# A fused attention and mixture-of-experts kernel: products with v from float16 parts, 240 slots per expert, weight conversion shared between two stages

## The chip, the cores and the metric

The kernel runs on one core of one Trainium2 chip, as one launch. The metric is the device time of one execution in microseconds (us); smaller is better. The core has a matrix engine (TensorE: PE for its products, PEld for its weight loads), three engines for elementwise work (VectorE, DVE; ScalarE, ACT; GpSimd, POOL) and a queue engine (SyncE, SP) that issues most of the transfers. Each engine works through its own list of instructions in order, and semaphores hold it where it needs another's result.

## The reference

```
# attention, batch 2, 8 heads, 768 positions, head size 64
mask   = bucket(q) == bucket(k)          # 6 sign bits of x @ proj
scores = where(mask, q @ k.T / 8, -1e9)
x      = softmax(scores) @ v             # -> 1536 tokens of 512
# dense layer, 512 -> 2048 -> 512
h = x @ w_in;  x = (h * tanh(softplus(h))) @ w_out
# eight experts, 512 -> 1024 -> 512; each token goes to one of them
e   = argmax(cosine(x, expert_emb) / tau)
out = softmax(...)[e] * (relu(x @ w1[e]) @ w2[e])
```

Everything is float32 in the arguments and in the result.

## The kernel before

All products but one kind are made from float16 parts: each float32 operand is cut into a high part and a low part, and three float16 products (high by high, high by low, low by high) are added up in PSUM. The one exception is the product of the softmax numerators `p` with `v` (`pv`), which takes float32 operands. The kernel has three stages.

**Attention** (16 heads, one after another). The work of a head is cut into 6 steps, one for each tile of 128 keys; `g` counts the steps, 6 to a head, and each step has 6 positions. In a step TensorE makes the scores of one key tile (`score_unit`, L384 and L386, two halves of 384 queries each), one or two products for the row maxima of a head that comes 10 steps later (`max_unit`, L344 and L348; VectorE reduces each out of PSUM, two buffers, L345 and L349), and the two products of the tile of 3 steps before with `v` (`pv`, L401). ScalarE makes `p` from the scores (L389). `AT` says at which position, counted from a head's first step, each of the other pieces is issued: the cut of q and k into parts (`hi`, `lo0`, `lo1`), the transposing transfers on SP's queue (`in_x`, `in_m`), the bucket bits (`args`, `bits`), and for each pair of heads the normalisation (`inv`, `scale`, `xhi`, `xlo`). `run_all` writes this order out, and a helper keeps each engine to it.

**Dense layer** (3 chunks of 512 tokens, 16 tiles of 128 hidden columns, so 48 tiles `G`). For each tile TensorE makes 12 products `up` (L767) and, three tiles later, 12 products with `w_out` (L825). Between them four ScalarE functions, three VectorE operations (L846, L851, L867), one ScalarE copy (L860) and one GpSimd subtraction (L861) make the two parts of `g`. `w_in` and `w_out` come as float64 and are converted by `w1_work`: 32 pieces of 128 x 512, each with three VectorE operations (L694, L696, L676: these are the steps of the generator), then ScalarE and GpSimd operations for the two parts (`w1_free` in the attention, `w1_busy` in the dense layer, where the low parts of `w_out` are left to VectorE). `CVS` says how many steps of that generator are taken in each step `g` of the attention; the rest is taken in the dense layer by `fill`, which is called 6 times a tile and takes one step when the generator is due (what it yields says how many calls must pass). The conversion for expert 0 (`w2_work`, L1105 and L1106) is chained behind it.

**Experts**. A table in DRAM has `CAP` slots for each expert; tokens are scattered to it, and every expert works on all its slots: for each expert 96 products `up` with `CAP` columns (L1150) and 48 products `down` with 512 columns, whose weights are the hidden values of 128 slots (L1164). The weights of the next expert are loaded and cut meanwhile (L1087, L646, L647). If an expert had more tokens than `CAP`, a fallback loop over all experts and all tokens would run (`overflow`).

Of the kernel before, what the change touches and what calls it, by code (L numbers as in the profile page):

```python
# [11 lines left out]
F16 = mybir.dt.float16  # L12
# [8 lines left out]
P = 128  # L21
# [6 lines left out]
PB = 5  # L28
EMB0 = -2
BLANK = 4  # L30
CVS = ((5, 99, 1),)
LEAD = 5
UP = {95: 0, 99: 1}
TEND = 101
PRE = {96: 2, 97: 2, 98: 2}
RPB, CVB = 1, 3
STEP = 7
AT = dict(rows_t=-7, rows_in=-7, m_row=-22, bits=-90, max_end=-24, hi=-150, lo0=-130, lo1=-122, dup=-114, in_x=-116, in_m=-84, args=-91, load_kq=-190, load_v=-37, out0=50, out1=54, s_row=55, inv=77, r_out=79, r_in=91, scale=112, xhi=127, xlo=139)
GAP = dict(bits=1, max_end=1, inv=1)
STEPS = dict(bits=3, max_end=2, inv=2)  # L40
FROM = dict(rows_in=1, m_row=4, bits=3, max_end=1, hi=4, lo0=4, lo1=4, dup=4, in_x=4, in_m=4, rows_t=1, args=3, load_kq=6, load_v=2)
UNTIL = dict(rows_t=4, rows_in=4)
EVERY = dict(load_kq=(2, 0), load_v=(2, 0)) | {k: (2, 1) for k in ("inv", "r_out", "r_in", "scale", "xhi", "xlo")}
LAST = ("inv", "r_out", "r_in", "scale", "xhi", "xlo")
SP, MP, OP = 1, (1, 5, 11), (1, 5)
NBUF, NVB, KXB, KMB = 3, 2, 5, 4
# [97 lines left out]
class Attn:  # L144
    def __init__(self, tc, ctx, q, k, v, proj, ident, ones, xx, dt, rest):
# [42 lines left out]
        for i in range(PB):  # L188
            if i in (1, 2):
                p = self.two[:, (i - 1) * (S + 1) : i * (S + 1)]  # L190
            else:
                p = self.pp.tile([P, S + 1], F32, name=f"p{i}", bufs=1)
            nc.gpsimd.memset(p[:, S : S + 1], 1e-9 / S)
            self.PT.append(p)

# [131 lines left out]

    def load_v(self, b, h):
# [48 lines left out]
    def score_unit(self, b, h, t):  # L377
# [9 lines left out]
        p = self.PT[self.pt % PB]  # L387
# [4 lines left out]
    def pv(self, b, h, t, c):  # L392
# [7 lines left out]
        o = z["o", c][0:m, 0 : HS + c]  # L400
        nc.tensor.matmul(o, self.vn(b, h, t), z["p"][t][:, cs], start=(t == 0), stop=(t == NJ - 1))  # L401

    def wide(self, b, h, tag, bufs):

        last = b == B - 1 and h >= H - 2
        name = tag
        pool, tag, bufs = (self.rest_pools[0], "stg", None) if last else (self.ou, tag, bufs)
        return pool.tile([P, S + 1], F32, tag=tag, name=f"{name}_{b}_{h}", bufs=bufs)

    def out(self, b, h, c):  # L410
# [13 lines left out]
        if i:  # L424
            self.nc.scalar.copy(z["s"][:, cs], o[0:1, 0:HS])

# [40 lines left out]
    def run_all(self, bs, hook=None):  # L467
# [47 lines left out]
        for n in range(N):  # L515
            for name, at in AT.items():
# [6 lines left out]
                if name in GAP:  # L523
# [56 lines left out]
CAP = 256  # L580
# [19 lines left out]
class Moe:  # L600
# [32 lines left out]
    def blank(self, tp, i):  # L633
# [6 lines left out]
        n = E0 * CAP // P // 16  # L640
        dst = self.xs[i * n * P : (i + 1) * n * P, :].rearrange("(a p) c -> p a c", p=P)
        nc.sync.dma_start(dst, self.z[:, None, :].to_broadcast([P, n, ROW]))
# [22 lines left out]
    def w1_work(self):  # L665
# [18 lines left out]
        for k in range(2 * NF1 + 1):  # L684
            busy = self.busy
            if old:
                end()
                yield 1
            if k < 2 * NF1:
# [5 lines left out]
                yield 1  # L695
                nc.vector.scalar_tensor_tensor(x, high, 0xC0000000, x, op0=ALU.bitwise_and, op1=ALU.bitwise_or)  # L696
                yield 1
# [683 lines left out]
```

## Time and profile before

| | |
|---|---|
| runs of the kernel before | 687.63 us median of 3 (686.86 to 688.06) |
| the profiled execution | 688.07 us; its span, first to last instruction, 686.3 us |
| granted TensorE clock over the span | 0.996 |
| busy, share of the span | PE 98%, PEld 54%, DVE 64%, ACT 69%, POOL 22% |

Busy is the union of an engine's instructions; a share is an average over stages that have different limits, so it has to be read stage by stage. The span leaves out 1.8 us around the first and the last instruction.

### The profile page before, as it was taken

To read this page: it belongs to the slowest core of one execution; us is meant where nothing else is said; L and a number is where in the kernel's file an instruction comes from. 1 tells how busy PE (TensorE), PEld (TensorE's weight loads), DVE (VectorE), ACT (ScalarE), POOL (GpSimd) and SP (SyncE) were. 2 spreads that over 40 slices of the span, in tenths; PEclk is the share of its full clock that TensorE was granted. 3 is DMA by queue.
4 is the path that set the end of the run, shared out by engine and by line. 5 is a ranking of instruction groups with operands and counts; after the bars stand their busy time and mean duration, and the time that the engine had idled before them with its cause. 6 is when DMAs were issued, how large, how long until landed. Compare 5 with 4: busy or idle time off the path is not lost. (4 is left out here: it accounts for less than half of the span.)

```text
span 686.3 us, 10415 instructions
## 1 busy us (share of the span) xinstructions
PE 670.8 (98%) x3890; PEld 371.5 (54%) x3890; DVE 440.9 (64%) x747; ACT 472.2 (69%) x716; POOL 152.7 (22%) x166
## 2 busy tenths in 40 slices
PE   8899999999999999999999999999999999999994
PEld 4555555555555454444444444445476777666772
DVE  6877888898887546766675555445466565556520
ACT  5667677676766769999898778887655565555520
POOL 3131211121111122222243242532530011110011
PEclk9999999999999999999999999999999999999998
DMA  7276887978864412345031010310555999988500
GB/s 218 64 148 151 183 194 165 229 156 186 179 136 134 118 56 91 91 125 154 1 98 26 1 63 22 78 24 2 187 181 145 305 275 292 251 258 245 157 23 21
DMA packets 120939, 93.23 MB, mean 136 GB/s; under 512 B 87847, under 2 KB 100135, under 8 KB 120882
## 3 DMA queue, kind: packets, MB, share of 16 engines
q1 hardware_dynamic: 112610, 81.18, 45.7%
q0 software_dynamic: 2240, 6.31, 3.3%
q10 hardware_dynamic: 6032, 5.01, 2.8%
q8 instruction: 32, 0.52, 0.3%
q14 instruction: 25, 0.20, 0.1%
HBM read 63.47 MB, written 14.77 MB: 114 GB/s over the span
## 5 line engine op out<-in xcount | busy, mean ns | idle before, releaser
L401 PE MATMUL o<-p,vn 128*65 128x384 f32 (+3 forms) x384 | 153.3, 486 | 0.1
L767 PE MATMUL h<-xx,wi 128*128 128x512 f16 x576 | 131.3, 379 | 0.1
L825 PE MATMUL x<-wo,g 128*128 128x512 f16 x576 | 131.2, 379 | 0.0
L389 ACT ACTIVATE p<-s 128x768 f32<-128x768 f32 x96 | 77.5, 808 | 53.0 <-PE s L386 51.3
L825 PEld LDWEIGHTS <-g 128*128 128x128 f16 x576 | 56.2, 98 | 68.1 <-POOL g L861 0.3
L767 PEld LDWEIGHTS <-wi 128*128 128x128 f16 x576 | 56.0, 98 | 67.5 <-issue 0.8
L861 POOL TENSOR_TENSOR g<-w,g 128x512 f16<-128x512 f32 x47 | 55.1, 1173 | 149.6 <-ACT g L860 90.4
L1164 PE MATMUL y<-b,hh 128*128 128x512 f16 x384 | 84.2, 379 | 0.0
L1150 PEld LDWEIGHTS <-a 128*128 128x128 f16 x768 | 75.1, 98 | 10.4 <-issue 0.2
L345 DVE TENSOR_REDUCE mx<-ms 128x1 f32<-128x512 f32 x96 | 65.8, 688 | 15.8 <-PE ms L344 15.2
L1150 PE MATMUL h<-xt,a 128*128 128x256 f16 x672 | 74.5, 273 | 0.0
L867 DVE SCALAR_TENSOR_TENSOR w<-w,u 128x512 f32<-128x512 f32 x47 | 32.5, 692 | 64.0 <-ACT u L858 64.0
L401 PEld LDWEIGHTS o<-p,vn 128*65 128x65 f32 (+1 forms) x384 | 59.6, 163 | 24.8 <-issue 10.8
L1164 PEld LDWEIGHTS <-hh 128*128 128x128 f16 x384 | 37.6, 98 | 43.6
L846 DVE SCALAR_TENSOR_TENSOR t<-t,u 128x512 f32<-128x512 f32 x47 | 39.1, 832 | 22.2 <-ACT t L873 22.2
L647 DVE SCALAR_TENSOR_TENSOR b<-st,b 128x1024 f16<-128x1024 f32 x28 | 33.1, 1222 | 24.8 <-ACT b L646 24.5
L1169 POOL DMA_INDIRECT out_dram<-o,row x16 | 15.6, 973 | 150.1 <-ACT o L1168 128.9
L647 DVE SCALAR_TENSOR_TENSOR a<-st,a 128x1024 f16<-128x1024 f32 x28 | 34.3, 1226 | 21.9 <-ACT a L646 21.9
L386 PE MATMUL s<-tm 97*128 97x384 f16 x192 | 47.0, 325 | 0.0
L384 PE MATMUL s<-tx 128*128 128x384 f16 x192 | 46.8, 325 | 0.0
L349 DVE TENSOR_REDUCE mx<-ms 128x2 f32<-128x512 f32 x48 | 33.0, 688 | 16.0 <-PE ms L348 15.3
L1156 ACT ACTIVATE hh<-h 128x512 f16<-128x512 f32 x32 | 19.1, 596 | 34.2 <-PE h L1150 33.1
(185 smaller groups left out, 917.6 us busy)
## 6 DMA issues: line engine op xcount, KB each, us to landing
st<-in_moe_w_dram SPq DMA_DIRECT2D x32, 1024.0 KB, 6.2
stg<-in_moe_w_in_dram SPq DMA_DIRECT2D x16, 512.0 KB, 4.2
stg<-in_moe_w_out_dram SPq DMA_DIRECT2D x16, 512.0 KB, 4.3
xs<-zrow SPq DMA_DIRECT2D x16, 257.0 KB, 8.1
vn<-in_v_dram SPq DMA_DIRECT2D x16, 192.0 KB, 6.5
rb<-rd SPq DMA_DIRECT2D x16, 192.0 KB, 3.7
xr<-row SPq DMA_DIRECT2D x2, 1024.0 KB
kq<-in_k_dram ACTq DMA_DIRECT2D x5, 384.0 KB, 3.9
```

Source lines behind the costliest of these rows:

```text
L345: nc.vector.tensor_reduce(z["mx"][:, j, 0:1], s, axis=AX.X, op=ALU.max)
L384: nc.tensor.matmul(s[:, c, :], kq[:, 0, ts], kq[:, 1, c * HS : (c + 1) * HS], start=True, stop=False)
L386: nc.tensor.matmul(s[:, c, :], m[0:97, 0, ts], m[0:97, 1, c * HS : (c + 1) * HS], start=False, stop=True)
L389: nc.scalar.activation(p[:, 0:S].rearrange("p (c n) -> p c n", c=2), s, AF.Exp, scale=2.0**-11)
L401: nc.tensor.matmul(o, self.vn(b, h, t), z["p"][t][:, cs], start=(t == 0), stop=(t == NJ - 1))
L647: nc.vector.scalar_tensor_tensor(lo, src, sc, hi, op0=ALU.mult, op1=ALU.subtract)
L767: self.nc.tensor.matmul(h, self.wi[wu][:, k, fs], x[:, k, xs], start=(i == 0), stop=(i == 3 * NKT - 1))
L825: nc.tensor.matmul(x2[r], gf[:, gu, rs], self.wo[wu][:, f, :], start=(f == 0 and gu + wu == 0), stop=(f == NF1 - 1 and gu == 1))
L846: nc.vector.scalar_tensor_tensor(t1, t1, 0.75, u1, op0=ALU.add, op1=ALU.mult)
L861: nc.gpsimd.tensor_tensor(g[G - 1][:, 1, :], p1, g[G - 1][:, 0, :], op=ALU.subtract)
L1150: nc.tensor.matmul(h[:, v, :], W[0][wu][:, k, fs], xt[e][:, xu * NKT + k, :], start=(i == 0), stop=(i == 3 * NKT - 1))
L1164: nc.tensor.matmul(y[s], hs[F // 2][:, hu, F % 2, s * P : (s + 1) * P], W[1][wu][:, F, :], start=(F == 0 and hu + wu == 0), stop=(F == NF2 ...
```

## The change

1. `CAP` goes from 256 to 240, so an expert's slots are cut into 128 and 112. The products `up` have 240 columns; the second half of the products `down` has weights of 112 columns; the last 112 rows are given out by a smaller transfer.
2. For key tiles 1 and 4 of heads 2 to 15, `pv` is made from float16 parts: GpSimd cuts `v` (`v16`), ScalarE makes the high part of `p`, VectorE the low part (`p16`), and three float16 products take the place of one float32 product. The parts share one buffer, which also serves as a buffer of `p` for head 0; there are four buffers of `p` in place of five, and four of the transposed q and k (`KXB`) in place of five. To fit, `in_x`, `args`, `bits` and `in_m` are issued one step later.
3. `CVS` takes .58 steps of the weight conversion for each step of the attention in place of 1: int(99 x .58) - int(5 x .58) = 55 steps in place of 94, of 97. In the dense layer each step of the generator then waits for two calls of `fill` in place of one.
4. The last pair's normalisation uses the space of `w_out`'s last four tiles (`LATE`) in place of the staging buffers, and the 1e-9 of the denominator is multiplied in by a small GpSimd operation after the copy.

Changed lines (empty lines and context left out):

```diff
@@ constants @@
-PB = 5
+PB = 4
-CVS = ((5, 99, 1),)
+CVS = ((5, 99, .58),)
+LATE = 12
-AT = dict(rows_t=-7, rows_in=-7, m_row=-22, bits=-90, max_end=-24, hi=-150, lo0=-130, lo1=-122, dup=-114, in_x=-116, in_m=-84, args=-91, load_kq=-190, load_v=-37, out0=50, out1=54, s_row=55, inv=77, r_out=79, r_in=91, scale=112, xhi=127, xlo=139)
+AT = dict(rows_t=-7, rows_in=-7, m_row=-22, bits=-84, max_end=-24, hi=-150, lo0=-130, lo1=-122, dup=-114, in_x=-110, in_m=-78, args=-85, load_kq=-190, load_v=-37, out0=50, out1=54, s_row=55, inv=77, r_out=79, r_in=91, scale=112, v16=-16, p16=(9, 13), xhi=127, xlo=139)
-FROM = dict(rows_in=1, m_row=4, bits=3, max_end=1, hi=4, lo0=4, lo1=4, dup=4, in_x=4, in_m=4, rows_t=1, args=3, load_kq=6, load_v=2)
+FROM = dict(v16=2, p16=2, rows_in=1, m_row=4, bits=3, max_end=1, hi=4, lo0=4, lo1=4, dup=4, in_x=4, in_m=4, rows_t=1, args=3, load_kq=6, load_v=2)
-EVERY = dict(load_kq=(2, 0), load_v=(2, 0)) | {k: (2, 1) for k in ("inv", "r_out", "r_in", "scale", "xhi", "xlo")}
+EVERY = dict(v16=(2, 0), load_kq=(2, 0), load_v=(2, 0)) | {k: (2, 1) for k in ("inv", "r_out", "r_in", "scale", "xhi", "xlo")}
-NBUF, NVB, KXB, KMB = 3, 2, 5, 4
+NBUF, NVB, KXB, KMB = 3, 2, 4, 4
+T16 = (1, 4)
+N16 = range(2, 16)
@@ Attn.__init__ @@
-            if i in (1, 2):
-                p = self.two[:, (i - 1) * (S + 1) : i * (S + 1)]
+            if i >= 2:
+                p = self.two[:, (i - 2) * (S + 1) : (i - 1) * (S + 1)]
-            nc.gpsimd.memset(p[:, S : S + 1], 1e-9 / S)
+            nc.gpsimd.memset(p[:, S : S + 1], 1.0)
+        self.V16 = []
+        for i in range(NVB):
+            vh, vl = (cp.tile([P, len(T16), 65 + P], F16, name=f"v{u}{i}") for u in "hl")
+            nc.gpsimd.memset(vh, 0.0)
+            nc.gpsimd.memset(vh[:, :, 64:66], 1.0)
+            nc.gpsimd.memset(vl, 0.0)
+            self.V16.append((vh, vl))
+        both = cp.tile([P, 2 * (S + 1)], F16, name="p16")
+        self.P16 = [both[:, u * (S + 1) : (u + 1) * (S + 1)] for u in range(2)]
+        self.PX = both.bitcast(F32)
+        nc.gpsimd.memset(self.PX[:, S : S + 1], 1.0)
@@ Attn (new v16, p16) @@
+    def v16(self, b, h):
+        nc = self.nc
+        if b * H + h == N16[0]:
+            for u in range(2):
+                nc.gpsimd.memset(self.P16[u][:, S : S + 1], 1.0 - u)
+        for i in range(2):
+            for k, t in enumerate(T16):
+                vh, vl = (x[:, k, i * 129 : i * 129 + D] for x in self.V16[(b * H + h) // 2 % NVB])
+                v = self.vn(b, h + i)[:, t]
+                nc.gpsimd.tensor_copy(vh, v)
+                nc.gpsimd.tensor_tensor(vl, v, vh, op=ALU.subtract)
+    def p16(self, b, h, t, u):
+        hi, lo = (x[:, 0:S] for x in self.P16)
+        p = self.Z[b, h]["p"][t][:, 0:S]
+        if u == 0:
+            self.nc.scalar.copy(hi, p)
+        else:
+            self.nc.vector.tensor_tensor(lo, p, hi, op=ALU.subtract)
@@ Attn.score_unit @@
-        p = self.PT[self.pt % PB]
+        p = self.PX if self.pt in (0, NJ - 1) else self.PT[(self.pt - 1 - (self.pt >= NJ)) % PB]
@@ Attn.pv, Attn.wide @@
+        if t in T16 and b * H + h in N16:
+            V = [x[:, T16.index(t), i * 65 : i * 65 + m] for x in self.V16[(b * H + h) // 2 % NVB]]
+            for vu, pu in ((0, 0), (1, 0), (0, 1)):
+                nc.tensor.matmul(o, V[vu], self.P16[pu][:, cs], start=(t == 0 and vu + pu == 0), stop=(t == NJ - 1 and pu == 1))
+            return
-        name = tag
-        pool, tag, bufs = (self.rest_pools[0], "stg", None) if last else (self.ou, tag, bufs)
-        return pool.tile([P, S + 1], F32, tag=tag, name=f"{name}_{b}_{h}", bufs=bufs)
+        if last:
+            w = self.rest_pools[0][tag != "ou"][:, LATE:NF1, :]
+            return w.rearrange("p f d -> p (f d)").bitcast(F32)[:, 0 : S + 1]
+        return self.ou.tile([P, S + 1], F32, tag=tag, name=f"{tag}_{b}_{h}", bufs=bufs)
@@ Attn.out @@
+            if c:
+                self.nc.gpsimd.tensor_scalar(z["w"][:, S : S + 1], z["w"][:, S : S + 1], 1e-9 / S, None, op0=ALU.mult)
@@ Attn.run_all @@
-                if name in GAP:
+                if name == "p16":
+                    for t in T16:
+                        for u in range(2):
+                            put(n, 6 * t + at[u], self.p16, t, u)
+                elif name in GAP:
@@ constants @@
-CAP = 256
+CAP = 240
+CS = (slice(0, P), slice(P, CAP))
@@ Moe.blank @@
-        n = E0 * CAP // P // 16
-        dst = self.xs[i * n * P : (i + 1) * n * P, :].rearrange("(a p) c -> p a c", p=P)
-        nc.sync.dma_start(dst, self.z[:, None, :].to_broadcast([P, n, ROW]))
+        if i < E0 * CAP // P:
+            nc.sync.dma_start(self.xs[i * P : (i + 1) * P, :], self.z)
@@ Moe.w1_work @@
-                yield 1
+                yield 2 if busy else 1
-                yield 1
+                yield 2 if busy else 1
-                yield 1
+                yield 2 if busy else 1
@@ Moe.early @@
-        nc.sync.dma_start(self.row0, self.xs[0:CAP, 0:DM].rearrange("(s p) c -> p s c", p=P))
+        for s, c in enumerate(CS):
+            nc.sync.dma_start(self.row0[0 : c.stop - c.start, s, :], self.xs[c, 0:DM])
@@ Moe.first @@
-            for s in range(2):
-                self.nc.tensor.matmul(x[:, v, s * P : (s + 1) * P], row0[:, s, cs], self.ident, start=False, stop=False)
+            for s, c in enumerate(CS):
+                n = c.stop - c.start
+                self.nc.tensor.matmul(x[:, v, c], row0[0:n, s, cs], self.ident[0:n, 0:n], start=False, stop=False)
@@ Moe.moe2: number @@
-                nc.sync.dma_start(rows[e][s], self.xs[e * CAP + s * P : e * CAP + (s + 1) * P, DM:ROW])
+                nc.sync.dma_start(rows[e][s][0 : CS[s].stop - CS[s].start], self.xs[e * CAP + CS[s].start : e * CAP + CS[s].stop, DM:ROW])
@@ Moe.moe2: down, give @@
-                    nc.tensor.matmul(y[s], hs[F // 2][:, hu, F % 2, s * P : (s + 1) * P], W[1][wu][:, F, :], start=(F == 0 and hu + wu == 0), stop=(F == NF2 - 1 and hu == 1))
+                    nc.tensor.matmul(y[s][0 : CS[s].stop - CS[s].start], hs[F // 2][:, hu, F % 2, CS[s]], W[1][wu][:, F, :], start=(F == 0 and hu + wu == 0), stop=(F == NF2 - 1 and hu == 1))
-            nc.scalar.activation(o, y[s], AF.Copy, scale=rows[e][s][:, 0:1].bitcast(F32))
-            nc.gpsimd.indirect_dma_start(self.a["out"], bass.IndirectOffsetOnAxis(ap=rows[e][s][:, 1:].bitcast(I32), axis=0), o, None, bounds_check=NT - 1, oob_is_err=False)
+            n = CS[s].stop - CS[s].start
+            nc.scalar.activation(o[0:n], y[s][0:n], AF.Copy, scale=rows[e][s][0:n, 0:1].bitcast(F32))
+            nc.gpsimd.indirect_dma_start(self.a["out"], bass.IndirectOffsetOnAxis(ap=rows[e][s][0:n, 1:].bitcast(I32), axis=0), o[0:n], None, bounds_check=NT - 1, oob_is_err=False)
@@ moe_attn @@
-            at = Attn(tc, c2, a["q"], a["k"], a["v"], a["proj"], ident, moe.ones, xx, dt, (moe.stg, tl))
+            at = Attn(tc, c2, a["q"], a["k"], a["v"], a["proj"], ident, moe.ones, xx, dt, (moe.wo, tl))
```

## Rows read from the trace of the kernel before

**Rows 1.** Busy time of each engine in stretches (us, PE, PEld, DVE, ACT, POOL, clock, DMA)
```profile
28.00:252.00 224.00, 223.19 (x1134) 122.62 (x1133) 176.52 (x348) 157.72 (x238) 40.10 (x35) 1.00 0.67 154
263.00:364.00 101.00, 101.00 (x470) 45.78 (x469) 68.50 (x85) 93.00 (x152) 30.63 (x27) 1.00 0.33 96
510.00:677.00 167.00, 166.98 (x1157) 112.82 (x1154) 90.66 (x98) 82.56 (x104) 17.89 (x19) 1.00 0.77 212
```

**Rows 2.** The same view for two heads of the attention, one after the other
```profile
108.10:122.06 13.96, 13.96 (x74) 7.86 (x73) 13.11 (x25) 10.92 (x17) 2.31 (x2) 1.00 0.75 172
122.06:136.01 13.95, 13.95 (x73) 7.77 (x72) 11.08 (x25) 9.58 (x14) 2.50 (x2) 1.00 0.97 224
```

**Rows 3.** Timeline of PE in the attention (start, length, instruction)
```profile
129.94 0.81 PE L401 MATMUL o<-p,vn 128*128 128x384 f32 x2
...
130.59 0.38 PE L348 MATMUL ms<-tm 96*128 96x256 f16 x2
...
131.46 0.49 PE L384 MATMUL s<-tx 128*128 128x384 f16 x2
...
132.11 0.38 PE L344 MATMUL ms<-tm 96*128 96x512 f16 x1
```

**Rows 4.** Timeline of PE in the last expert
```profile
656.28 10.64 PE L1150 MATMUL h<-xt,a 128*128 128x256 f16 x96
...
666.76 10.52 PE L1164 MATMUL y<-b,hh 128*128 128x512 f16 x48
```

**Rows 5.** Weight loads by line and shape (count, busy us, mean ns, idle before)
```profile
L1164 PEld LDWEIGHTS <-hh 128*128 128x128 f16 x384 | 37.6, 98 | 43.6
...
L401 PEld LDWEIGHTS o<-p,vn 128*65 128x65 f32 x192 | 25.5, 137 | 14.3 <-issue 6.5 <-ACT su L425 1.1
```

**Rows 6.** DVE by line, 108 to 192 us, six heads
```profile
L696 DVE SCALAR_TENSOR_TENSOR cv<-stg,cv 128x512 uint32<-128x512 uint32 x12 | 10.6, 881 | 0.0
L676 DVE SCALAR_TENSOR_TENSOR cv<-stg,cv 128x512 uint32<-128x512 uint32 x12 | 8.3, 692 | 0.0
...
L694 DVE TENSOR_SCALAR cv<-stg 128x512 uint32<-128x512 uint32 x12 | 5.0, 417 | 0.0
...
L465 DVE TENSOR_TENSOR xx<-rb,xx 128x768 f16<-128x768 f32 x3 | 2.8, 946 | 0.0
```

**Rows 7.** ACT by line, the same stretch
```profile
L704 ACT ACTIVATE cv<-cv 128x512 f32<-128x512 f32 x12 | 7.6, 630 | 1.1
...
L462 ACT CAST xx<-rb 128x768 f16<-128x768 f32 x3 | 2.4, 815 | 0.0
```

**Rows 8.** POOL by line, the same stretch
```profile
L705 POOL TENSOR_TENSOR wo<-cv,wo 128x512 f16<-128x512 f32 x6 | 6.9, 1157 | 38.2 <-ACT cv L704 38.2
```

**Rows 9.** SP's queue: the transposing transfer for head 12 is issued
```profile
161.10 1.84 SPq L247 DMA_TRANSPOSE tm<-kq  x1
```

**Rows 10.** Timeline of PE: the first product that reads it
```profile
169.14 0.38 PE L344 MATMUL ms<-tm 96*128 96x512 f16 x1
```

**Rows 11.** All twelve such transfers, from issue to landing
```profile
DMA to landing us min/median/max: 3.1/4.4/5.2
```

**Rows 12.** Timeline at the start of the dense layer
```profile
263.37 5.34 PE L825 MATMUL x<-wo,g 128*128 128x512 f16 x24
...
264.63 1.16 POOL L861 TENSOR_TENSOR g<-w,g 128x512 f16<-128x512 f32 x1 [3.07 <-ACT g L860]
```

**Rows 13.** DVE by line, 256 to 340 us, eighteen tiles of the dense layer
```profile
L867 DVE SCALAR_TENSOR_TENSOR w<-w,u 128x512 f32<-128x512 f32 x18 | 12.5, 693 | 17.1 <-ACT u L858 17.1
L846 DVE SCALAR_TENSOR_TENSOR t<-t,u 128x512 f32<-128x512 f32 x17 | 12.1, 713 | 3.2 <-ACT t L873 3.2
L851 DVE SCALAR_TENSOR_TENSOR w<-t,h 128x512 f32<-128x512 f32 x17 | 11.7, 687 | 0.6
L1106 DVE SCALAR_TENSOR_TENSOR a<-st,a 128x512 f16<-128x512 f32 x8 | 10.2, 1278 | 2.5 <-ACT a L1105 2.5
```

**Rows 14.** ACT in the experts: the cut of the next expert's weights (page, part 5)
```profile
L646 ACT ACTIVATE a<-st 128x1024 f16<-128x1024 f32 x28 | 29.4, 1049 | 4.4 <-DMA st<-in_moe_w_dram 4.4
```


## The prediction

> **What bounds the kernel now.** I read the busy time by stage first. In the attention TensorE is busy 223.2 of 224 us, in the dense layer 101 of 101, in the experts 167 of 167, at the full clock [rows 1]. So the time is the sum of TensorE's products, and a product that becomes shorter shortens the kernel, as long as the other engines keep up. How near they are is the second thing to read, in the same view head by head: a head takes 13.96 us, and every other head (the one in which a pair is normalised) has VectorE busy 13.11 of them, the next one 11.08; ScalarE is at 10.9 and 9.6 [rows 2]. In the first part of the dense layer ScalarE is nearest, 93 of 101, with VectorE at 68.5 [rows 1]. Third, the timeline of TensorE gives what a product costs from start to start (a duration holds the drain too, which overlaps the next).
>
> **Float16 products with v.** Each float32 product is two instructions. From its first start to the next instruction is 130.59 - 129.94 = 0.65 us. The four float16 score products, with the same 384 columns, take 132.11 - 131.46 = 0.65 us, so 0.1625 each [rows 3]. Three of these are 0.49 us, and 0.16 us is saved at each product. There are 14 heads x 2 tiles x 2 halves = 56: **-9.1 us**. The weight loads of the three are hidden as those of the scores are. Bounds: no saving only if ScalarE or VectorE takes over (below).
>
> **240 slots.** 96 products of 256 columns take 10.64 us, 0.1108 each; 48 of 512 columns take 10.52, 0.2192 each [rows 4]. So a column costs (0.2192 - 0.1108) / 256 = 0.42 ns, and 16 columns less in 8 x 96 = 768 products are **-5.2 us**. The products that bring expert 0's rows together shrink at the same price, 32 of them by 16 columns and 4 by 32: **-0.3 us**. The products `down` keep 512 columns. Half of them, 192, now load 112 columns of weights. The trace has no such load in float16; it shows 98 ns for 128 columns behind 219 ns of product, and 137 ns for 65 columns of float32, also behind products [rows 4, 5]. Below, this costs nothing; above, if no load could be hidden, 192 x 0.098 = 18.8 us. I take 0, because the float32 loads, also of a broken width, are covered by products only slightly longer. The weight transfers must come 3% faster. ScalarE waited for them 4.4 us in 28 cuts of this kind [rows 14], no product waited, and the transfer engines are 77% busy [rows 1], so I take 0 for that too.
>
> The Trainium skill (TensorE: Matmul & The Clock Gate, Weight-path perf modes) says that the fast weight load needs exactly 128 weights that are not float32, so the loads of 112 and 65 columns lose it. The same page gives a plain load as columns / 1.2, an estimate of 93 ns for 112. By that the load would still lie behind the 219 ns and the sum stay; no row here shows a float16 load of that width.
>
> **What VectorE gets in the attention.** A head loses 6 - 3.5 = 2.5 conversion steps, of (881 + 692 + 417) / 3 = 663 ns: -1.67 us. It gains two low parts of `p`; `xlo` has the same form, 128x768 float16 from float32, at 946 ns: +1.89 [rows 6]. So the full head goes from 13.11 to 13.3 us of work, and the new head is 13.96 - 4 x 0.16 = 13.3 us long; the light head has 11.3. VectorE is exactly full in every other head. ScalarE loses 0.84 conversions of two operations at 0.63 and gains two high parts at the 815 ns of `xhi` [rows 7]: +0.6, 11.5 of 13.3.
>
> VectorE now also waits. Each low part comes behind a high part that ScalarE makes after the scores and, in the heavy heads, after two copies of the previous result; behind it on VectorE stand the next cut of q and k and the next row maximum, and TensorE waits for that maximum with two buffers. In the new order `args` takes one of these just before a step with two maxima. Below, the light heads absorb all of it: 0. Above, each low part waits 0.7 us, so 1.4 in each of the five heavy heads between head 4 and head 12 and nothing in the light ones, which have 2 us free: 5 x 1.4 = 7 us. I put it near the lower end, at **+2.0 us**: TensorE may run two maxima ahead, which is longer than one such wait.
>
> **Queues.** `in_m` is issued one step, 13.3 / 6 = 2.2 us, later. The tightest transfer that I found (head 12) was issued at 161.10 and read at 169.14, 8.0 us; that leaves 5.8, and the slowest landing of the twelve took 5.2 [rows 9 to 11]. So it is hidden, with 0.6 us over; if that were gone, TensorE would stall by the excess once a head. `in_x` and `args` move together and keep their distance. `in_x` with four buffers waits for the scores of four heads before, issued half a step earlier; SP passes there in time. GpSimd's 8 small cuts of `v` a pair are at most the 1.16 us of a 512-column subtraction each [rows 8], 9 us in 27, on an engine busy 2.5 in 14 [rows 2]: hidden.
>
> **The conversion moved to the dense layer.** 39 steps, 13 to 14 pieces, come at about three steps a tile, so one piece a tile for the first 14 tiles. They bring their own loads on SP, under transfer engines at 33% [rows 1]; those wait at worst behind the last pair's row transfers and have two pieces of lead. Expert 0's weights, which were cut in these tiles, come later, into tiles where `g` is far ahead. The 24 products of a tile take 5.2 us [rows 12]. ScalarE was at 93 / 101 of that, 4.8 us, with 0.6 for a cut in most tiles, and gets 0.6 for a piece: no more than now. VectorE has 693 + 713 + 687 = 2.1 us of its own [rows 13], plus three steps (2.0 [rows 6]), plus for a piece of `w_out` a low part of 0.7 to 1.28: 4.1 to 5.4. So the pace holds, barely. What is not covered is the start: the second tile's low part ends at 265.79, and the third of its products, 265.96 + 2 x 0.216, starts at 266.4 [rows 12]: 0.6 us to spare, while tiles 0 and 1 now each bring a high part of 0.63 on ScalarE. Below 0; above, the rival below. I take **+1.0 us**.
>
> The ends (first 28 us, last expert's tail) keep their chains; the added fills on GpSimd at the start lie in its idle time. Sum: -9.1 - 5.2 - 0.3 + 2.0 + 1.0 = -11.6. The profiled execution, 688.07, goes to 676.5 (the 1.8 us around the span stay); the median of the runs is 0.4 lower, so the forecast for it is **676.0 us**.
>
> **Rivals.**
> - *Nothing is lost* (the two waits stay covered): 687.63 - 14.6 = 673.0. For it: every share above stays at or under 100%. Chance 0.14.
> - *VectorE sets the pace of the heads*: the full 7 us, and 1 in the dense layer: 681.0. For it: 13.3 of 13.3 us; against it: the light heads. Chance 0.18.
> - *VectorE sets the pace of the first 14 dense tiles, and the kernel is slower.* The low parts of expert 0's weights take 1278 ns, an operation of the same shape and float32 inputs 693 [rows 13]; the long ones ran beside GpSimd. If the two long steps of each piece stretch by 0.6 and the low part is 1.28, a tile has 2.1 + 2.0 + 1.2 + 1.28 = 6.6 us on VectorE, 1.4 over the 5.2. Fourteen tiles are 19.6 us less about 1 to spare: 676.0 - 1 + 18.6 = 693.6. It decides from 6.2 us a tile: the rest gains 12.6, and (12.6 + 1) / 14 = 1.0 above the 5.2. Against: `w_out`, 10 of the 14, leaves GpSimd no work, and at 5.2 us GpSimd is idle most of a tile (30.6 of 101 [rows 1]). The Trainium skill (GPSIMD Engine Reference, Specifications) says that GpSimd shares its SBUF interfaces with VectorE, in contention with instructions that have two SBUF inputs; the 1278 against 693 ns agree. Chance 0.06 that it is slower by this, 0.03 that it ends at no change, 0.04 for a smaller part of it, between 680 and 686.
> - *Loads of 112 columns are not hidden*: +18.8, 694.8. For it: no row shows such a load; against it: [rows 5]. Chance 0.02.
> - *The fallback runs.* Counting the reference's choices gives 187, 240, 173, 231, 194, 181, 187, 143 tokens: the fullest expert fills its 240 slots exactly. One more and 96 tiles of tokens go through all experts, over 1000 us by [rows 4]. 0.01.
> - *My forecast*, 1 to 5 us lost: 674 to 678.5, chance 0.52.
>
> **Numbers.** Likeliest 676.0. The range, 672.5 to 683, holds the forecast, the two rivals on its sides and half of the smaller part of the third. A measurement here can tell 0.2%, 1.4 us, so 686.3 and 689.0 are the limits: faster 0.88, same 0.03, slower 0.09.
>
> **What would show it.** In the profile after: the length of a head (13.3 us; more means VectorE or ScalarE), VectorE's idle before the low part of `p` and who ended it, TensorE's waits for the row maxima, the distance of `g`'s low part to its product in tiles 1 to 3, 96 products `up` in 10.0 us, and idle time before the products with 112-column weights. Wrong it would be if TensorE shows idle time in the heads over 0.5 us each or in the first 14 dense tiles.

## The result: 1.3% slower, and the profile after

The changed kernel takes 695.76 us (median of 6 runs, 695.0 to 697.95), the one before 687.49 beside it (6 runs, 686.41 to 688.06): a ratio of **1.0127 [1.0115, 1.0138]**. The forecast was 676.0, faster. The profiled execution took 697.0 us, its span is 695.1 and the granted clock 0.991.

Cut at the first product `up` of the dense layer and at the first of the experts, the two spans compare so (us):

| | before | after | difference | forecast |
|---|---|---|---|---|
| until the first `up` of the dense layer | 243.96 | 248.65 | +4.7 | -7.1 |
| from there to the first `up` of the experts | 266.24 | 275.94 | +9.7 | +0.7 |
| experts and end | 176.10 | 170.56 | -5.5 | -5.2 |

The experts did what was forecast, the attention and the dense layer did not. (The forecast's 0.3 for expert 0's gather stands in the second line.)

The busy time of three heads, to be read beside [rows 2] (columns: length, PE, PEld, DVE, ACT, POOL, clock, DMA share, GB/s):

```profile
80.69:97.72 17.03, 15.22 (x77) 8.44 (x76) 12.96 (x24) 11.74 (x18) 1.77 (x2) 0.90 0.51 125
111.66:126.13 14.47, 13.54 (x77) 7.89 (x76) 12.77 (x24) 11.18 (x18) 2.07 (x2) 1.00 0.54 131
126.13:139.86 13.73, 13.67 (x78) 7.69 (x76) 11.88 (x25) 9.85 (x16) 5.92 (x10) 1.00 0.98 213
```

A head should have come to 13.3 us. One is at 17.0, one at 14.5, one at 13.7, and in the first two TensorE is not busy throughout. (Of the 17.0 some 1.7 us, (1 - 0.90) x 17.03, are a lower granted clock; the last section shows it.) But no other engine is full either: VectorE has 12.96 of 17.03 and ScalarE 11.74. A share does not explain this; the waits of TensorE do (engine, line, releaser: us in total, times, longest):

```profile
PE o L443 <- ACT su L468: 6.7, 7, 1.8
PE h L816 <- DVE w L900: 3.1, 5, 0.9
PE x L874 <- DVE w L900: 2.4, 1, 2.4
```

The first line is the attention: the product with `v` (L443) waits for ScalarE's copy of a result out of PSUM (L468). There are two result buffers `ps_o`, one for each half of the queries, so the product of tile 0 of a head can start only when the previous head's half has been copied out. The longest of these waits, on TensorE and then on ScalarE:

```profile
90.81 0.86 PE L443 MATMUL o<-p,vn 128*65 128x385 f32 x2 [1.81 <-ACT su L468]
```

```profile
87.15 0.47 ACT L468 COPY su<-o 1x384 f32<-1x384 f32 x1
...
87.68 0.83 ACT L361 CAST p<-p 128x768 f16<-128x768 f32 x1
88.42 0.62 ACT L752 ACTIVATE wi<-cv 128x512 f16<-128x512 f32 x1
89.14 0.63 ACT L753 ACTIVATE cv<-cv 128x512 f32<-128x512 f32 x1
89.79 0.48 ACT L466 COPY ou<-o 64x385 f32<-64x385 f32 x1
90.29 0.47 ACT L468 COPY su<-o 1x384 f32<-1x384 f32 x1
```

Between the copies of the first half and those of the second ScalarE makes the new high part of `p` (L361) and then the two operations of a conversion piece. TensorE stands until the last copy ends at 90.76. In the kernel before, nothing stood between them in the same head:

```profile
86.95 0.47 ACT L425 COPY su<-o 1x384 f32<-1x384 f32 x1
87.44 0.48 ACT L423 COPY ou<-o 64x385 f32<-64x385 f32 x1
87.93 0.47 ACT L425 COPY su<-o 1x384 f32<-1x384 f32 x1
```

From the first half's last copy to the second half's it was 0.98 us there. In the changed kernel it is 1.7 to 3.1 us in all seven such heads before the last pair: L361 stands between in each, a conversion piece in two of them (the ones with 3.1 and 3.0 us).

The first part of the dense layer, in the same view as [rows 1]:

```profile
267.75:288.00 20.25, 16.54 (x76) 7.31 (x75) 19.88 (x27) 15.68 (x26) 9.61 (x9) 1.00 0.37 117
...
329.00:350.00 21.00, 21.00 (x99) 9.45 (x97) 14.18 (x19) 19.57 (x31) 4.67 (x4) 1.00 0.28 87
```

Here VectorE is full, 19.88 of 20.25 us, and TensorE is not; from 329, past the moved pieces, TensorE is full again. VectorE's lines there, 256 to 350 us, beside [rows 13] and the conversion steps of [rows 6], and GpSimd's new line:

```profile
L916 DVE SCALAR_TENSOR_TENSOR w<-w,u 128x512 f32<-128x512 f32 x16 | 14.9, 930 | 5.6 <-ACT u L907 5.6
L745 DVE SCALAR_TENSOR_TENSOR cv<-stg,cv 128x512 uint32<-128x512 uint32 x14 | 12.8, 918 | 0.0
L895 DVE SCALAR_TENSOR_TENSOR t<-t,u 128x512 f32<-128x512 f32 x16 | 12.4, 774 | 1.6 <-ACT t L922 1.6
L900 DVE SCALAR_TENSOR_TENSOR w<-t,h 128x512 f32<-128x512 f32 x16 | 11.0, 687 | 0.6
L725 DVE SCALAR_TENSOR_TENSOR cv<-stg,cv 128x512 uint32<-128x512 uint32 x14 | 10.9, 779 | 0.0
L761 DVE SCALAR_TENSOR_TENSOR wo<-cv,wo 128x512 f16<-128x512 f32 x10 | 8.9, 890 | 1.2 <-ACT wo L759 1.2
L743 DVE TENSOR_SCALAR cv<-stg 128x512 uint32<-128x512 uint32 x13 | 8.9, 684 | 0.0
```

```profile
L763 POOL TENSOR_SCALAR cv<-cv 128x512 f32<-128x512 f32 x4 | 7.6, 1912 | 0.1
```

The steps did not only move, they became longer: 417 to 684 ns, 692 to 779, 881 to 918, and the layer's own operation 693 to 930. Added up by these means, a tile with a piece of `w_out` has 0.930 + 0.774 + 0.687 + 0.918 + 0.779 + 0.684 + 0.890 = 5.7 us on VectorE, more than TensorE's 5.2.

A mean hides two lengths here. Of the 13 operations L743, ten took 0.42 to 0.45 us and three 1.40 to 1.84; the three lay beside GpSimd's subtraction L910, which the dense layer always had:

```profile
287.95 0.42 DVE L743 TENSOR_SCALAR cv<-stg 128x512 uint32<-128x512 uint32 x1
...
294.17 1.16 POOL L910 TENSOR_TENSOR g<-w,g 128x512 f16<-128x512 f32 x1 [0.43 <-ACT g L909]
294.21 1.41 DVE L743 TENSOR_SCALAR cv<-stg 128x512 uint32<-128x512 uint32 x1
```

The experts' products `down` with the narrow weights, and their loads, by shape:

```profile
L1215 PE MATMUL y<-b,hh 128*112 128x512 f16 x192 | 42.7, 379 | 0.0
```

```profile
L1215 PEld LDWEIGHTS <-hh 128*112 128x112 f16 x192 | 25.0, 130 | 16.7
...
L1215 PEld LDWEIGHTS <-hh 128*128 128x128 f16 x192 | 18.8, 98 | 20.8
```

A load of 112 columns takes 130 ns and one of 128 takes 98, and no product waits for either: behind 219 ns both are hidden.

### The profile page after: what moved, and what is told of

Read it like the earlier page. It is cut to its first block, busy times and chain, and to the rows that moved or that the text cites. A ratio compares the mean times of both kernels' runs of the same rounds, so it can differ in the third digit from the quotient of the medians.

```text
span 695.1 us, 10684 instructions
## 1 busy us (share of the span) xinstructions
PE 664.4 (96%) x3946; PEld 378.4 (54%) x3946; DVE 481.3 (69%) x784; ACT 482.3 (69%) x731; POOL 178.1 (26%) x233
## 5 line engine op out<-in xcount | busy, mean ns | idle before, releaser
L443 PE MATMUL o<-p,vn 128*65 128x384 f32 (+3 forms) x272 | 109.7, 489 | 7.7 <-ACT su L468 6.7
L910 POOL TENSOR_TENSOR g<-w,g 128x512 f16<-128x512 f32 x47 | 55.6, 1183 | 143.4 <-ACT g L909 81.8
L1215 PE MATMUL y<-b,hh 128*128 128x512 f16 (+1 forms) x384 | 84.2, 379 | 0.0
L1201 PE MATMUL h<-xt,a 128*128 128x240 f16 x672 | 70.0, 266 | 0.0
L916 DVE SCALAR_TENSOR_TENSOR w<-w,u 128x512 f32<-128x512 f32 x47 | 36.3, 773 | 44.3 <-ACT u L907 44.3
L1215 PEld LDWEIGHTS <-hh 128*128 128x128 f16 (+1 forms) x384 | 43.7, 114 | 37.6
L443 PEld LDWEIGHTS o<-p,vn 128*65 128x65 f32 (+1 forms) x272 | 41.8, 164 | 27.8 <-ACT su L468 9.2
L895 DVE SCALAR_TENSOR_TENSOR t<-t,u 128x512 f32<-128x512 f32 x47 | 40.9, 871 | 12.0 <-ACT t L922 12.0
L922 ACT ACTIVATE t<-w,bias 128x512 f32<-128x512 f32 x47 | 33.5, 714 | 12.8 <-DVE w L916 12.8
L1220 ACT ACTIVATE o<-y,row 128x512 f32<-128x512 f32 (+1 forms) x16 | 11.0, 687 | 44.4 <-PE y L1215 26.1
```

Of the source, the lines that this page charges most:

```text
L895: nc.vector.scalar_tensor_tensor(t1, t1, 0.75, u1, op0=ALU.add, op1=ALU.mult)
L910: nc.gpsimd.tensor_tensor(g[G - 1][:, 1, :], p1, g[G - 1][:, 0, :], op=ALU.subtract)
L1201: nc.tensor.matmul(h[:, v, :], W[0][wu][:, k, fs], xt[e][:, xu * NKT + k, :], start=(i == 0), stop=(i == 3 * NKT - 1))
L1215: nc.tensor.matmul(y[s][0 : CS[s].stop - CS[s].start], hs[F // 2][:, hu, F % 2, CS[s]], W[1][wu][:, F, :], start=(F == 0 and hu + wu == 0) ...
```

## The experiments

Each ratio is to the kernel before, run beside it on the same chip (its medians there 687.4 to 687.7). "Attention" is the time of the first `up` of the dense layer, "dense" the time from it to the first `up` of the experts, both in the span.

| run | float16 tiles | conversion in the attention | attention | dense | median us | ratio |
|---|---|---|---|---|---|---|
| before | none | all | 243.96 | 266.24 | | 1 |
| after | 1, 4 | 55 steps | 248.65 | 275.94 | 695.76 | 1.0127 |
| e1_slots | none | all | 244.03 | 266.02 | 683.19 | 0.9938 [0.9921, 0.9955] |
| e5_moved | none | 55 steps | 248.11 | 274.51 | 700.97 | 1.0199 [1.0182, 1.0216] |
| e9_even | none | half, evenly | 244.91 | 276.71 | 698.49 | 1.0152 [1.0135, 1.0169] |
| e4_nopool | 1, 4 | 55 steps | 248.01 | 272.03 | 693.47 | 1.0090 [1.0073, 1.0107] |
| e3_order | 1, 4 | 55 steps | 250.20 | 274.15 | 699.01 | 1.0167 [1.0150, 1.0184] |
| e6_tiles03 | 0, 3 | 55 steps | 246.21 | 274.57 | 694.56 | 1.0105 [1.0089, 1.0122] |
| e10_noparts | 1, 4 | 55 steps | 238.20 | 274.67 | (below) | |
| e12_pool | 1, 4 | 55 steps | 241.06 | 274.50 | 689.37 | 1.0027 [1.0016, 1.0039] |
| e7_back03 | 0, 3 | all | 245.54 | 265.71 | 684.35 | 0.9962 [0.9948, 0.9976] |
| e8_one | 0 | all | 248.37 | 266.02 | 687.93 | 1.0007 [0.9997, 1.0017] |
| e13_both14 | 1, 4 | all | 258.61 | 265.71 | 695.18 | 1.0106 [1.0089, 1.0123] |
| **e11_three5** | 3 | all | 238.99 | 265.71 | **679.06** | **0.9873 [0.9857, 0.9890]** |

### One part alone

**e1_slots: the kernel before with 240 slots.** Only the hunks of `CAP`.

```diff
-CAP = 256
+CAP = 240
```

> The kernel before with 240 slots alone. Theory: the experts are bound by TensorE, and the loads of 112 columns are hidden, so 768 products lose 6.8 ns each and the kernel gains 5 to 6 us: about 682 us, 96 products up in 10.0 us, TensorE without idle time in the experts. Rival (loads of 112 columns show): 192 products grow, up to 18.8 us more than that.

683.19, 4.2 us less (4.9 in the span of the profiled execution), somewhat under the 5 to 6 expected; why is not shown. No product waits for a load, so the narrow loads cost nothing.

**e5_moved: the kernel before with the moved conversion alone** (with it the space of the last pair, which it needs).

```diff
-CVS = ((5, 99, 1),)
+CVS = ((5, 99, .58),)
-                yield 1
+                yield 2 if busy else 1
```

> The kernel before with the moved conversion alone (0.58 steps a step of the attention, two calls in the dense layer, the last pair's space in w_out). Theory: the attention, where VectorE had time to spare, gains nothing, the dense layer loses 7 to 10 us as in the changed kernel: 694 to 698 us. Rival (the dense layer loses only because the attention hands over late): under 689 us.

The move by itself costs 13.6 us in the median, more than expected. In the span it is 8.3 in the dense layer, and 4.2 in the attention, although that has fewer steps to do. At .58 steps for each step of a head the pieces fall at other places in every head. In two of the seven pairs of heads before the last a conversion piece falls between the two halves' copies on ScalarE, which then stand 2.23 us apart and not 0.98; TensorE waits for a copy just twice (1.2 us in all), and once for the transfer `in_m` (1.6).

**e9_even: the same with half the conversion, three steps in each head,** at the same places.

```diff
-CVS = ((5, 99, .58),)
+CVS = ((5, 99, .5),)
```

> The kernel before with half a conversion step a step of the attention, so that each head has three, always at the same places; no float16 products with v. Theory (the 4 us that the attention lost with 0.58 come from conversion steps that fall elsewhere in each head): the attention takes 244 us again, without waits, and only the dense layer loses, 8 to 10 us: 696 to 699 us. Rival (fewer steps in the attention make SP's loads late anyway): attention 246 to 248 us, over 700 us.

As expected but for the last 1.0 us of the attention: it is back within that of the kernel before, with no conversion piece between the copies and no wait for them, so most of the 4.2 was where the steps fell, not how many there are. The dense layer loses more, 10.5, with more moved into it.

### What the dense layer waits for

**e4_nopool: after, with the low parts of `w_in` made by one VectorE operation in place of two of GpSimd,** in the dense layer alone.

```diff
-        if sc == 256.0:
-            self.lows.append(lambda: nc.vector.scalar_tensor_tensor(lo, w, sc, hi, op0=ALU.mult, op1=ALU.subtract))
-        else:
-            nc.gpsimd.tensor_scalar(w, w, sc, None, op0=ALU.mult)
-            nc.gpsimd.tensor_tensor(lo, w, hi, op=ALU.subtract)
+        self.lows.append(lambda: nc.vector.scalar_tensor_tensor(lo, w, sc, hi, op0=ALU.mult, op1=ALU.subtract))
```

> The changed kernel; in the dense layer the low parts of the pieces of w_in are made by one VectorE operation, as those of w_out are, and not by two GpSimd operations. Theory (VectorE is stretched while GpSimd works): the first 16 dense tiles get back 3 to 5 of the 6.6 us that they lost, about 691.5 us. Rival (the number of VectorE operations alone counts): four more operations of 0.7 us on VectorE, 695 to 698 us.

VectorE's lines of this run, 254 to 348 us:

```profile
L912 DVE SCALAR_TENSOR_TENSOR w<-w,u 128x512 f32<-128x512 f32 x17 | 18.5, 1087 | 6.6 <-ACT u L903 6.6
...
L760 DVE SCALAR_TENSOR_TENSOR wo<-cv,wo 128x512 f16<-128x512 f32 x10 | 9.9, 990 | 1.7 <-ACT wo L759 1.7
L725 DVE SCALAR_TENSOR_TENSOR cv<-stg,cv 128x512 uint32<-128x512 uint32 x14 | 9.6, 687 | 0.0
L745 DVE SCALAR_TENSOR_TENSOR cv<-stg,cv 128x512 uint32<-128x512 uint32 x14 | 9.5, 681 | 0.0
L743 DVE TENSOR_SCALAR cv<-stg 128x512 uint32<-128x512 uint32 x13 | 5.5, 422 | 0.0
```

VectorE has an operation more for each of these pieces, and yet the first 16 tiles take 80.5 us in place of 83.0 (76.4 before): without the two GpSimd operations beside them the steps are at 687, 681 and 422 ns again. So some 2.5 us went to these two, a little less than the 3 to 5 expected. The other 4.1 are not the moved work alone. GpSimd's subtraction is left, and now other operations lie beside it: seven of the 17 L912 took about 1.65 us and ten 0.69 to 0.70, five of the ten L760 about 1.3 and five 0.68. That lengthening adds up to some 9.8 us (7 x 0.96 + 5 x 0.62). At the short lengths a tile would have 3 x 0.69 + 0.687 + 0.681 + 0.422 + 0.68 = 4.5 us on VectorE, under the 5.2 (an estimate); no run took the subtraction away, so whether the pace would then hold is not shown. As it is VectorE shows 19.1 of 20 us here:

```profile
265.00:285.00 20.00, 18.44 (x85) 8.07 (x84) 19.14 (x29) 16.89 (x28) 5.15 (x6) 1.00 0.46 139
```

That VectorE slows beside a busy GpSimd agrees with the Trainium skill (GPSIMD Engine Reference, Specifications), which has the two share SBUF interfaces. The Trainium skill names there VectorE's instructions with two SBUF inputs or in a 2-port mode; the one that slowed most here, 417 to 684 ns, has one input, and no run shows its mode.

### What the attention waits for

**e3_order: after, with both parts of `p` made three positions later,** so that the high part stands behind the copies.

```diff
-p16=(9, 13)
+p16=(12, 16)
```

> The changed kernel with the high part of p issued three positions later, behind the copies of the previous head's result, and the low part three positions later. Theory (ScalarE's order): the copies come free earlier, TensorE no longer waits for the two result buffers (7.5 us of waits and the drains around them), and the attention ends 7 to 10 us earlier, about 687 us. Rival (VectorE is full): VectorE has the same work, so the heads stay at 13.7 to 14 us and the time within 2 us of 695.8.

My theory fell here: slower, not faster, and by more than the rival's 2 us too. The waits for the copies shrank to 1.8 us, as it said, but another kind came up:

```profile
PE ms L381 <- DVE mx L386: 8.6, 12, 1.0
...
PE o L443 <- ACT su L468: 1.8, 2, 0.9
```

The low part now comes late on VectorE (between 45 and 250 us VectorE waits 22.1 us for the high parts, 9.1 in the changed kernel), the row maximum stands behind it, and TensorE waits for the maxima's buffers 12 times. Moving the work within a head trades one wait for the other.

**e6_tiles03: after, with tiles 0 and 3.**

```diff
-T16 = (1, 4)
+T16 = (0, 3)
```

> The changed kernel with key tiles 0 and 3 made from float16 parts, not 1 and 4. Every engine has the same work; only the step of a head in which the parts are made differs: tile 0's high part comes in step 1, where ScalarE has little else, tile 3's behind the copies of the previous result. Theory (what is lost is the order on ScalarE and VectorE around the copies): the heads come down to 13.3 to 13.7 us, about 688 us. Rival (VectorE is full): nothing changes, 694 to 697 us.

2.4 us better in the attention, of which some 1.7 are the lower clock that this run's profile does not have there; in the median 1.2. So the rival's number came out, but not its cause: the waits are of the same kind and size, now before the float16 product of tile 0:

```profile
PE o L441 <- ACT su L468: 5.3, 6, 1.8
...
PE o L441 <- ACT ou L466: 2.3, 3, 1.1
```

**e10_noparts: after, without the instructions that make the parts of `p`.**

```diff
     def p16(self, b, h, t, u):
-        if u == 0:
-            self.nc.scalar.copy(hi, p)
-        else:
-            self.nc.vector.tensor_tensor(lo, p, hi, op=ALU.subtract)
+        pass
```

> The changed kernel without the instructions that make the float16 parts of the probabilities: two copies of 0.83 us on ScalarE and two subtractions on VectorE a head are left out, and the float16 products read buffers that are filled once (the output is not the reference's). TensorE's work is the same, instruction for instruction. Theory (these instructions fill ScalarE and VectorE, and TensorE waits for the copies of its results that stand behind them): the waits for the result buffers go, the first product of the dense layer stands near 239 us of the span (243.96 before, less 9.1, plus 4.1 for the moved conversion as the kernel with that alone showed), time 684 to 688 us. Rival (the shorter products reach the result buffers too soon whatever the other engines do, as in the run with tile 0 alone): first dense product at 246 to 249, time 693 to 697.

The first product of the dense layer comes at 238.20, 10.5 us earlier than in the changed kernel with the same products on TensorE. The waits for the copies fall from 7 to 2, in the two heads in which a conversion piece still stands between them:

```profile
PE o L438 <- ACT su L463: 1.9, 2, 0.9
```

So the shorter products are not to blame, what makes their operands is. (The tokens here are other ones, an expert gets more than its slots, and the fallback loop runs: 1907 us, of which only the attention is read. It also shows what that rival would have cost: about 1,220 us.)

**e12_pool: after, with the high part made by GpSimd.**

```diff
-            self.nc.scalar.copy(hi, p)
+            self.nc.gpsimd.tensor_copy(hi, p)
```

> The changed kernel with the high parts of the probabilities made by GpSimd instead of ScalarE. Theory (ScalarE's copies for the parts delay the copies of the results): the waits for the result buffers fall from 6.7 us to under 2, first dense product at 242 to 246 (248.65 in the changed kernel) and 689 to 693 us, unless the later low parts bring back the waits of the row maxima that the run with the parts behind the copies showed. Rival (VectorE is what is full, and a busy GpSimd stretches it): first dense product at 249 or later, 696 to 701.

One word moves 7.6 of the 10.5 us: 241.06, and 6.4 us in the median, as the theory had it or slightly better. GpSimd took 931 ns for a cast that takes ScalarE 0.83 us. TensorE's largest wait in the attention is now:

```profile
PE o L443 <- ACT su L468: 1.9, 2, 1.1
```

The two waits left are again those with a conversion piece between the copies. With e3, where the same work behind the copies took most of these waits away, it is the high part's place in front of ScalarE's copies that was the main cause in the attention. What of the other 2.9 us is the low part on VectorE was not tried apart.

### With the conversion back in the attention

**e7_back03: tiles 0 and 3, the whole conversion in the attention as before, 240 slots.** It is e6 with this undone (and the last pair's space with it):

```diff
-CVS = ((5, 99, .58),)
+CVS = ((5, 99, 1),)
-                yield 2 if busy else 1
+                yield 1
```

> As the run before this one, but with the whole conversion in the attention again, as in the kernel before (one step a step, one call in the dense layer, the last pair's space in the staging buffers). VectorE then has 15.0 and 13.0 us of work in a heavy and a light head, 14.0 in the mean, against 13.3 on TensorE. The dense layer takes 266 us again in both theories. If VectorE's amount sets the heads, they take about 14.0 us and nothing is won in the attention: 683 us. If only the order counts, the heads take 13.3 to 13.5: 675 us.

The dense layer is at 265.7 again, so its whole loss was the moved conversion. In the attention 1.6 us more than before are spent, against 9.1 that should be saved. The time is what was expected if VectorE's amount sets the heads, and VectorE is full:

```profile
80.00:94.00 14.00, 13.07 (x75) 7.59 (x74) 13.92 (x25) 11.91 (x19) 3.15 (x3) 1.00 0.66 187
```

But TensorE's waits name the copies far more than the row maxima:

```profile
PE o L441 <- ACT su L467: 4.2, 6, 0.9
...
PE o L441 <- ACT ou L465: 1.4, 1, 1.4
...
PE ms L381 <- DVE mx L386: 0.9, 2, 0.6
```

Some of ScalarE's copies waited for VectorE in turn (2.9 us, before L465). How much of the loss a full VectorE made is therefore not shown.

**e8_one: the same with tile 0 alone.**

```diff
-T16 = (0, 3)
+T16 = (0,)
```

> The whole conversion in the attention, 240 slots, and only key tile 0 from float16 parts: 28 products lose 0.16 us each (-4.6), VectorE has 14.0 and 12.0 us in a head of 13.63. Both theories: TensorE is the bound of nearly all heads, the dense layer as before, 678 to 680 us. If a single high and low part already holds up the heads, 683 us.

Missed by both: with half the products the attention is worse, 248.37. Two kinds of wait make up 6.8 us:

```profile
PE o L441 <- ACT su L467: 3.4, 6, 0.6
PE ms L381 <- DMA tm<-kq: 2.3, 3, 1.3
...
PE o L441 <- ACT ou L465: 1.1, 1, 1.1
```

The second line is the transfer `in_m`, issued one step later with four key buffers. It is worse than e7 only because it saves less: less the products' saving (4.5 and 9.1 us) the attention loses 9.0 us here and 10.7 in e7. Why half the parts cost nearly as much is not settled.

**e11_three5: tile 3 alone, the whole conversion in the attention, and the five key buffers and old steps of the loads,** for which one tile leaves space.

```diff
-T16 = (0,)
+T16 = (3,)
-NVB, KXB, KMB = 3, 2, 4, 4
+NVB, KXB, KMB = 3, 2, 5, 4
-bits=-84, in_x=-110, in_m=-78, args=-85
+bits=-90, in_x=-116, in_m=-84, args=-91
```

> 240 slots, the whole weight conversion in the attention as before, float16 products for tile 3 alone (the middle of a head, away from the hand-over of the result buffers), five key buffers and the loads at their old steps. Theory (half the float16 tiles, in a place that has slack, keep the saving): 28 products at 0.16 us each less is 4.5 us off the 683.2 of the kernel with 240 slots alone: 678 to 680.5, first dense product near 239.5 to 241. Rival (any part made on ScalarE and VectorE beside the whole conversion gives its gain back, as with tile 0): 683 to 688, first dense product at 244 or later.

679.06, the best of all, 1.3% under the kernel before. The saving of 28 products, 4.5 us, arrives in full (the attention goes from 243.96 to 238.99), and TensorE is busy without a gap in these two heads and waits for nothing from 45 us to the end of the attention:

```profile
78.98:106.27 27.29, 27.29 (x150) 15.59 (x149) 25.89 (x51) 21.84 (x33) 6.75 (x9) 1.00 0.79 190
```

VectorE has 25.89 of 27.29 us here, nearly full, and holds nothing up. Against e8 it changes two things, the tile and the loads; which of them does more was not tried apart.

**e13_both14: tiles 1 and 4, the whole conversion in the attention, both parts of `p` by GpSimd.**

```diff
-            self.nc.scalar.copy(hi, p)
+            self.nc.gpsimd.tensor_copy(hi, p)
-            self.nc.vector.tensor_tensor(lo, p, hi, op=ALU.subtract)
+            self.nc.gpsimd.tensor_tensor(lo, p, hi, op=ALU.subtract)
```

> The changed kernel (240 slots, float16 products for tiles 1 and 4) with the whole weight conversion back in the attention and both parts of the probabilities made by GpSimd. Theory (what was lost was VectorE's and ScalarE's time only; GpSimd had half of the span free, and its cast of a tile took 0.93 us): VectorE has about 24 of 26.6 us a pair of heads, ScalarE 20; the first dense product stands at 235 to 239, the dense layer is back at 266, time 674 to 679, at or below the run with tile 3 alone (679.06). Rival (GpSimd's chain of a cast and a subtraction a tile, behind its steps of the conversion, comes too late for the products, and its traffic stretches VectorE): TensorE waits for the low parts or for the row maxima, first dense product at 241 to 248, time 681 to 688.

The rival, and worse than it said: 258.61. GpSimd's subtraction takes twice VectorE's 0.95 us, and VectorE's conversion step L724 goes from 692 ns [rows 6] to 1194:

```profile
L363 POOL TENSOR_TENSOR p<-p,p 128x768 f16<-128x768 f32 x24 | 43.4, 1808 | 1.4
```

```profile
L724 DVE SCALAR_TENSOR_TENSOR cv<-stg,cv 128x512 uint32<-128x512 uint32 x23 | 27.5, 1194 | 0.0
```

```profile
PE ms L381 <- DMA tm<-kq: 8.2, 8, 2.6
PE ms L381 <- DVE mx L386: 6.5, 6, 1.4
```

VectorE comes late with the row maxima; and the transfers that TensorE waits for, issued one step later in this kernel too, are now the largest wait.

## Why the prediction was wrong

**The products, -9.1: right.** In the changed kernel three float16 products take 143.38 - 142.90 = 0.48 us from start to start, as forecast:

```profile
142.90 0.33 PE L441 MATMUL o<-p,vh 128*128 128x384 f16 x1
...
143.38 0.38 PE L385 MATMUL ms<-tm 96*128 96x256 f16 x2
```

With nothing to prepare, e10 has the attention 5.8 us shorter in spite of the moved conversion, and e11 shows the saving of one tile in full.

**The slots, -5.2 and -0.3: right.** The experts became 5.5 us shorter; 240 slots alone gave 4.2 in the median, three quarters of the sum. The load of 112 columns was dearer than one of 128, 130 against 98 ns, and as forecast it is hidden. That a load of other than 128 columns loses the fast path agrees with the Trainium skill (TensorE: Matmul & The Clock Gate, Weight-path perf modes). The estimate of 93 ns, from the Trainium skill's columns / 1.2 on that page, was too low.

**The wait in the attention, +2.0, at most 7: this step failed.** The attention gave back 4.7 + 9.1 = 13.8 us. The forecast weighed VectorE against the head's length and followed only the row maxima; it saw the high part only behind "two copies of the previous result", not in front of the next two, and took ScalarE, at "11.5 of 13.3", as having room. What it left out is that TensorE's product of tile 0 waits for just these copies, with two result buffers, one per half. By the runs, of the 13.8 us some 10.5 come from making the parts (248.65 against 238.20), and 7.6 of these go when ScalarE no longer makes the high part. (Up to 1.7 of either number is the lower clock after the longest wait, which e10 and e12 do not have in the attention.) The other 3.3 are what is lost with no parts made (238.20 against 243.96 - 9.1); the moved conversion alone lost 4.2, and taken evenly 1.0, because at .58 some of its pieces come between the copies too. The forecast had counted fewer steps in the attention as a pure relief.

**VectorE as the pace of the heads: not what happened.** In the changed kernel VectorE has 12.96 of 17.03 us. With the whole conversion back it has 13.92 of 14.00 (e7), and even there the waits name ScalarE's copies first; at 25.89 of 27.29 (e11) TensorE waits for nothing.

**The dense layer, +1.0: this step failed too.** It lost 9.7 us: 6.6 in the first 16 tiles, 8.5 by the last of the 48, and 1.2 more in the routing, where the granted clock was 0.66 over 518 to 523 us. Without the move the loss is gone (e7), and the move alone loses 8.3 (e5). This is the mechanism of the slower rival, VectorE stretched beside GpSimd as the pace of the first tiles, at about a third to a half of its 18.6. The forecast's "So the pace holds, barely" failed on the lengths: it had 4.1 to 5.4 us of VectorE in a tile, with the steps at 2.0 and the layer's own operations at 2.1, from rows in which GpSimd was mostly idle beside them. Measured were 2.4 and 2.4, and 5.7 in all with the low part of a `w_out` piece, over the 5.2 of TensorE. The two GpSimd operations that moved along account for 2.5 us (e4); the rest is the moved work and its lengthening beside the subtraction that was there before, not split further.

**The queues: right for the time, by luck.** `in_m` had 0.6 us over by the forecast, with 5.2 us as the slowest landing. In the changed kernel head 9's transfer took 7.3 us and landed at 131.21, and its reader started at 131.25, after a wait of the weight load of 0.45 us. In e8 and e13 it is a wait of TensorE.

**The sum.** In the span: +4.7 + 9.7 - 5.5 = +8.9, measured 695.1 - 686.3 = 8.8.

## What to carry to other kernels

When another engine prepares an operand for a shorter product, look at what stands behind the new instruction in that engine's order and who waits for it, above all a copy that frees one of few PSUM buffers: an engine at three quarters can still hold TensorE in every second head. Work moved to a stage where TensorE is at 100% and another engine at 68% is not free there, the less so if a third engine's operations lengthen that one's; it is first to be tried alone. And a change of several parts can hold one that is right: here 240 slots and one float16 tile in the middle of the head gave 1.3%, where all parts together lost 1.3%.

## What the hardware showed beside this

- After the wait of 1.81 us in the attention the granted clock went to its lower level (1.2 GHz of 2.4) for most of the stretch from 92 to 96 us, once more in the routing:

```profile
92.00:96.00 4.00, 4.00 (x15) 2.04 (x14) 2.43 (x6) 2.57 (x4) 0.00 (x0) 0.57 0.49 149
...
518.00:523.00 5.00, 4.43 (x40) 3.48 (x40) 3.06 (x19) 0.29 (x2) 1.53 (x2) 0.66 0.01 3
```

In e6 a wait of 1.8 us and one of 2.4 us were followed by no such stretch, so a wait's length alone does not tell it here. At 0.57 over 4.00 us the first stretch cost about 1.7 us of TensorE's time.
- A scaling of 128x512 float32 took GpSimd 1912 ns, in the dense layer beside a full VectorE; a cast of 128x768 to float16, in the attention, took only 931. What of this is the kind of operation and what the neighbour was not tried apart.
